# Sliding-window attention with a dense layer behind it: for 17 of 23 sessions the attention weights become the stationary operand, v with a column of ones the moving one, and x is transposed by SyncE's DMA

## The chip, the cores and the metric

The kernel runs on one core of one Trainium2 chip. Its time is the device time of one execution in microseconds (us); lower is better. TensorE (PE in the profile, its weight loads PEld) multiplies matrices, VectorE (DVE) and ScalarE (ACT) work element by element and read PSUM, GpSimd (POOL) here mostly issues the loads that convert float32 to bfloat16, and SyncE (SP) issues stores and DMA transposes.

## The reference

```python
# q, k, v: (8 batches, 8 heads, 576 tokens, 64)
scores = q @ k.transpose(0, 1, 3, 2) / sqrt(64)
scores = where(abs(i - j) <= 32, scores, -1e9)        # a band of 65 keys per query
attn   = softmax(scores)
x      = (attn @ v).transpose(0, 2, 1, 3).reshape(4608, 512)
h      = x @ w_in                                      # w_in: 512 x 2048
g      = where(h >= 1, h, where(h <= -1, 0, (h + 1)**2 / 4))
out    = g @ w_out                                     # w_out: 2048 x 512, float32
```

## The kernel before

All matrices are bfloat16 in SBUF; sums are float32 in PSUM. x is kept transposed: `xT` has its 512 features in four blocks of 128 partitions and its tokens along the free axis, in a ring of 4 x 576 tokens. `gT` is g transposed in the same manner, in four homes of 256 tokens.

**The main loop** runs over 144 steps `a` and after that over 16 more. A step projects hidden features of some tokens (`hp`, from `w_in` and `xT`: L609 for 256 features of 256 tokens, L630 for 128 features of 512 tokens in steps 56 to 135), then ACT and DVE make g of it (L648 to L655). A step also issues some of the matmuls of `g @ w_out` (`unit`, L563), whose number is written out by hand in the list `units`. Everything is in an order written out by hand; nothing is reordered by a scheduler, and each engine takes its instructions in order.

**Attention** runs ahead of the projection as a stream. From batch 1 on, the keys of all batches are cut into blocks of 64. Session k consists of `stream_sums(k)` and `stream_scores(k + 1)`; the list `sl` says in which step it runs. For the sessions that matter here the steps are: k = 6 in step 33, 7 in 36, 8 in 39, 9 in 44, 10 in 48, 11 in 51, 12 in 59, 13 in 66, 14 in 71, 15 in 74, 16 in 81, 17 in 87, 18 in 95, 19 in 99, 20 in 108, 21 in 111, 22 in 123. `stream_scores` multiplies k with q (L283) into PSUM, ACT takes the exponential (L289, L292) into the ring `wt` [keys of a block on 64 partitions, twice; queries along the free axis], DVE masks it (L200) and adds the two halves that belong to the same query into `rows` (L299). `stream_sums(k)` covers 192 queries: for each block of 64 keys it loads v as the stationary operand and moves `wt` past it (L366), so that the result comes out with the features of v on the partitions, which is what `xT` wants; and it moves `rows` past a block of ones to get the sums of the softmax on all partitions. Four 64x64 tiles of TensorE are used: `a`, the half of the partitions that the keys stand on, and `h`, the half of the partitions that the result goes to. `normal` then takes the reciprocal of the sums on ACT as exp(-ln(sum)) (L317, L320, L321), and its last step, a multiply on DVE that writes `xT` (L325), is put in the list `muls`, which `flush` issues at the start of the next step.

**Loads.** `load_nat` (L103) issues the loads of a batch's q and k on GpSimd's queue, `xpose` (L193) turns each with a DMA transpose on SP's queue once it has landed, `load_v` (L111) loads v. After the transpose of k, GpSimd copies two columns of kT to `gate` (L668); the copy waits until that transpose has landed, and the loads of v come behind it in GpSimd's order. Stores of results (`out_dram<-osb`, L571) are on SP's queue too. Tokens of batch b stand at 576 b in the ring; session k writes 192 tokens from 576 + 736 + 192 (k - 6) on. The first step that reads tokens of a session is 40 for k = 6 and 7, 48 for k = 8, 56 for k = 9 to 11, 72 for 12 and 13, 88 for 14 to 16, 104 for 17 to 19, 120 for 20 and 21, and 136 for 22.

Of the kernel before, what the change touches and what calls it, by code (L numbers as in the profile page):

```python
# [7 lines left out]
FP = mybir.dt.float32  # L8
BF = mybir.dt.bfloat16
# [5 lines left out]
def kernel(  # L15
# [19 lines left out]
    nc = tc.nc  # L35
    B, H, S, D = q.shape
    NT, DM, DFF = out.shape[0], 512, 2048
    NY = H // 2
    NC = S // 64
# [3 lines left out]
    TURN = 2 * NC  # L43
    STREAMS = (0, NC, 2), (NC, (B - 1) * NC, 3)
    RING = 4 * S
    PAD = 32
    WIDE = 56, 136
    LONG = 2
    SPLIT = range(20, 25)

    const = ctx.enter_context(tc.tile_pool(name="const", bufs=1))
    nat = ctx.enter_context(tc.tile_pool(name="nat", bufs=2))
# [9 lines left out]
    def two_banks(pool):  # L62
        return pool.tile([128, 2, 512], FP, name="bb", tag="bb")
# [8 lines left out]
    w_out = const.tile([128, 16, DM], BF, name="w_out")  # L72
    xT = const.tile([128, NY, RING], BF, name="xT")
    gT = const.tile([128, 16, 4, 256], BF, name="gT")
    qTs = [const.tile([128, PAD + NY * S], BF, name=f"qT{i}") for i in range(3)]

    ctx.enter_context(tc.manual_schedule())
# [7 lines left out]
    def load_half(half, t, h, eng=None, x=None):  # L85

        src, dst, nm = ((q, qn, "qh"), (k, kn, "kh"))[t]
        if (0, half) not in dst:
            dst[0, half] = early.tile([128, 2, S], BF, name=nm, tag=nm, bufs=2) if x is None else x
        (eng or nc.gpsimd).dma_start(out=dst[0, half][:, h], in_=src[0].rearrange(  # L90
            "(h y) (l p j) d -> h l p y (j d)", h=2, l=2, p=32)[h][half])

# [12 lines left out]

    def load_v(b, n):
        if b not in vn:
            vn[b] = nat.tile([128, 2 * NC, 2, D], BF, name="vn", tag="vn", bufs=3)
        h, a = divmod(n, 2)
        y = NY * h + 2 * a  # L110
        nc.gpsimd.dma_start(out=vn[b][64 * a:64 * a + 64, :, h], in_=v[b, y:y + 2].rearrange("y s d -> (y s) d")  # L111
                            .rearrange("(c r) d -> r c d", r=64))

    def load_w_in(c0, c1, h, parts=(0, 64)):
# [46 lines left out]
    def qkT(b, t):  # L161
        if t == 0:
            return qTs[b % 3][:, PAD:]
        if b not in kT:
            kT[b] = ktp.tile([128, NY * S], BF, name="kT")
        return kT[b]
# [98 lines left out]
    def stream_scores(k, eng, pool=ps_s):  # L265

        assert eng is not None
        s, gs = turns[k]
        m = len(gs)
        r0 = (gs[0] - s) % TURN  # L270
        ps = two_banks(pool)
        sp = list(spare()) if m == 3 else None

        def place(h, y, n):
            return sp[h][:, 1, 128 * y:128 * y + 128] if n == 2 else ps[:, h, 256 * y + 128 * n:256 * y + 128 * n + 128]

        for y, n in [(y, n) for y in range(2) for n in range(min(m, 2))] + [(y, 2) for y in range(2) if m == 3]:
            for a in range(2):
                for h in range(2):
                    b, c = 1 + gs[n] // NC, gs[n] % NC  # L280
                    lo, hi = 32 * (c == 0), TAIL if c == NC - 1 else 128
                    s0 = S * (y + 2 * a) + 64 * c
                    nc.tensor.matmul(place(h, y, n)[HD[a], lo:hi], kT[b][HD[h], s0:s0 + 64],  # L283
                                     qTs[b % 3][HD[h], PAD + s0 - 32 + lo:PAD + s0 - 32 + hi],
                                     start=True, stop=True, skip_group_check=True)
        w0 = 128 * r0
        lo, hi = 32 * (gs[0] % NC == 0), 128 * m - 32 * (gs[-1] % NC == NC - 1)
        cut = min(hi, 256)
        A.activation(wt[:, :, w0 + lo:w0 + cut], ps.rearrange("p h (y j) -> p (h y) j", y=2)[:, :, lo:cut], AF.Exp,  # L289
                     scale=D ** -0.5)  # L290
        for h in (1, 0) if m == 3 else ():
            A.activation(wt[:, 2 * h:2 * h + 2, w0 + 256:w0 + hi],  # L292
                         sp[h][:, 1].rearrange("p (y j) -> p y j", y=2)[:, :, :hi - 256], AF.Exp, scale=D ** -0.5)
        mask(eng, wt[:, :, w0 + lo:w0 + hi], mask4.rearrange("p (m j) -> p m j", m=4)[:, :, lo:hi])
        M = turn_of(k)
        r = rows[64 * gs[0] - 32] = ptp.tile([128, 4, 192], BF, name="rows", bufs=2)
        if r0:
            x = wt[:, :, w0 - 64:w0 - 64 + 128 * M].rearrange("p m (n e j) -> p m n e j", n=M, e=2)
            V.tensor_add(r[:, :, :64 * M].rearrange("p m (n j) -> p m n j", n=M), x[:, :, :, 0], x[:, :, :, 1])  # L299
        else:  # L300
            V.tensor_add(r[:, :, :64], wt[:, :, 128 * TURN - 64:], wt[:, :, :64])
            x = wt[:, :, 64:64 + 128 * (M - 1)].rearrange("p m (n e j) -> p m n e j", n=M - 1, e=2)
            V.tensor_add(r[:, :, 64:64 * M].rearrange("p m (n j) -> p m n j", n=M - 1), x[:, :, :, 0], x[:, :, :, 1])

    def turn_of(k):

        return next(m for s, e, m in STREAMS if s == turns[k][0])
# [3 lines left out]
    def normal(bb, w, parts, more=None):  # L311
# [14 lines left out]
                                                                   rc[:, :, :D0].rearrange(like, y=2)[:, :, :, x0:x1]))  # L326
        return end

    def stream_sums(k, pool=ps_n):

        bb = two_banks(pool)
        s, m, lo, hi = ranges[k]
        w = hi - lo
        t = 64 * s + 64 * m * ((lo - 64 * s + 32) // (64 * m)) - 32
        r, i = (rows[t], lo - t) if t in rows else (wt, 128 * ((t - 64 * s) // 64 % TURN) + 64)
        more = list(spare()) if w > 128 else None
        cut = min(4 * w, 512) - 2 * w
        todo = []
        for y in range(2):
            for g in range(max(s, lo // 64 - 1), min(hi // 64 + 1, (B - 1) * NC)):  # L340
                b, c = 1 + g // NC, g % NC
                u = 64 * g - 32
                q0, q1 = max(lo, u, S * (b - 1)), min(hi, u + 128, S * b)
                if q0 < q1:
                    todo.append(((b, NC * y + c), 2, y * w + q0 - lo, y * w + q1 - lo,
                                 lambda a, h, y=y, j=128 * ((g - s) % TURN) - u, q0=q0, q1=q1: wt[HD[a], 2 * h + y, j + q0:j + q1]))
        if more is None:
            todo.insert(0, (None, 2, 2 * w, 4 * w, lambda a, h: r[HD[a], 2 * h:2 * h + 2, i:i + w]))
        else:
            def ends(n0, n1):  # L350
                def get(a, h):
                    if w == 192:
                        return r[HD[a], 2 * h:2 * h + 2].rearrange("p y j -> p (y j)")[:, n0:n1]
                    return r[HD[a], 2 * h + n0 // w, i + n0 % w:i + n0 % w + n1 - n0]
                return get
            todo += [(None, 2, 2 * w + c0, 2 * w + c1, ends(c0, c1)) for c0, c1 in spans(0, cut, w)]
            todo += [(None, None, c0 - cut, c1 - cut, ends(c0, c1)) for c0, c1 in spans(cut, 2 * w, w)]
        seen = set()
        for c, where, c0, c1, p in todo:
            for a in range(2):  # L360
                for h in range(2):
                    o = bb[HD[h], a, c0:c1] if where else more[a][HD[h], 0, c0:c1]
                    if not c and more is None:
                        o = o.rearrange("p (y j) -> p y j", y=2)
                    key = (a, h, where)
                    nc.tensor.matmul(o, vn[c[0]][HD[a], c[1], h] if c else ones[HD[a]],  # L366
                                     p(a, h), start=key not in seen, stop=True, skip_group_check=True)
                    seen.add(key)
        t0 = S + lo
        cut = min(w, RING - t0 % RING)  # L370
        return normal(bb, w, [(x0, x1, (t0 + x0) % RING) for x0, x1 in ((0, cut), (cut, w)) if x0 < x1], more)
# [5 lines left out]
    def sums(b, y1, lo, hi, pool=ps_n):  # L377
# [23 lines left out]
        for n, (c, c0, c1, p) in enumerate(todo):  # L401
            o = D0 if c is None else 0
            for a in range(2):
                for h in range(2):
                    nc.tensor.matmul(bb[HD[h], a, o + c0:o + c1], ones[HD[a]] if c is None else vn[b][HD[a], c, h],
                                     p(a, h), start=n == 0, stop=True, skip_group_check=True)

        def end():
# [121 lines left out]
    for t, a in enumerate([7, 16]):  # L530
        xps.setdefault(a, []).append((2, t))
    for b in range(LONG + 1, B):
        a = [19, 26, 37, 60, 84][b - 3]
        for t in range(2):
            loads.setdefault(a + t, []).append((b, t))
        for t in range(2):
            xps.setdefault([[23, 24], [33, 34], [46, 48], [65, 69], [89, 91]][b - 3][t], []).append((b, t))

    op = {}

# [76 lines left out]
    for a in range(NF * NB + 2 * NF):  # L617
# [46 lines left out]
        run(a + 0.5)  # L664
        for x in xps.get(a, []):
            xpose(*x)
            if x[1]:
                P.tensor_copy(gate, qkT(x[0], 1)[:, 0:2])  # L668
                for n in range(4):
                    load_v(x[0], n)  # L670

# [29 lines left out]
```

## Time and profile before

| | us |
|---|---|
| three runs | 303.43, 303.51, 302.79; median 303.43 |
| span of the profiled execution | 303.0 (no other time of that execution is given; the three runs lie within 0.5 around it) |
| TensorE busy | 293.1 (97%) |
| VectorE, ScalarE, GpSimd busy | 232.0, 203.4, 78.8 |
| DMA moved | 35.66 MB |

Busy time is the time in which an engine has an instruction in work. In rows of groups the columns are line, engine, operation, tiles, shapes and count, then busy time in us and mean ns of one, then the idle time just before them and what ended it. In rows of the timeline they are start, length, engine, line, operation, count, and in brackets the idle time before and its releaser. In rows of waits they are who waited for whom, us in all, times, longest. Rows of SPq and POOL with DMA in them show the issue of a transfer, not its landing; the landing stands in a row of its own.

### The profile page before, as it was taken

To read this page: it belongs to the slowest core of one execution; us is meant where nothing else is said; L and a number is where in the kernel's file an instruction comes from. 1 tells how busy PE (TensorE), PEld (TensorE's weight loads), DVE (VectorE), ACT (ScalarE), POOL (GpSimd) and SP (SyncE) were. 2 spreads that over 40 slices of the span, in tenths; PEclk is the share of its full clock that TensorE was granted. 3 is DMA by queue.
4 is the path that set the end of the run, shared out by engine and by line. 5 is a ranking of instruction groups with operands and counts; after the bars stand their busy time and mean duration, and the time that the engine had idled before them with its cause. 6 is when DMAs were issued, how large, how long until landed. Compare 5 with 4: busy or idle time off the path is not lost.

```text
span 303.0 us, 7769 instructions
## 1 busy us (share of the span) xinstructions
PE 293.1 (97%) x3244; PEld 172.2 (57%) x3244; DVE 232.0 (77%) x361; ACT 203.4 (67%) x383; POOL 78.8 (26%) x98
## 2 busy tenths in 40 slices
PE   8788999999999999999999999999999999999995
PEld 3466888876665766644444444444444444446644
DVE  4269789989987889898988989688978887546700
ACT  3678696757786777766878487777578547685301
POOL 8794740090073046055046000050000000000000
PEclk9999999999999999999999999999999999999999
DMA  9999999999999999999989900697111110000121
GB/s 151 180 180 199 187 186 154 225 151 156 185 65 147 178 171 145 166 188 147 195 119 161 159 17 22 131 137 73 38 35 38 35 37 35 37 35 35 38 104 69
DMA packets 137971, 35.66 MB, mean 118 GB/s; under 512 B 122320, under 2 KB 134352, under 8 KB 137936
## 3 DMA queue, kind: packets, MB, share of 16 engines
q0 software_dynamic: 103056, 18.06, 81.0%
q1 hardware_dynamic: 34736, 16.81, 23.9%
q8 instruction: 25, 0.41, 0.6%
q10 hardware_dynamic: 144, 0.29, 0.4%
q14 instruction: 10, 0.08, 0.1%
HBM read 36.70 MB, written 9.44 MB: 152 GB/s over the span
## 4 chain that ended last, share of the span: by engine, by line
PE 82%; DMA 7%; POOL 5%; DVE 2%; ACT 2%; issue 1%; POOLq 0%; ACTq 0%; DVEq 0%
PE op L563 34%; PE hp L630 23%; PE hp L609 14%; PE op L581 4%; PE bb L366 3%; DMA w_out<-in_moe_w_out_dram 3%; DMA vn<-in_v_dram 2%; POOL w_in L116 2%; DMA w_in<-in_moe_w_in_dram 2%; POOL vn L111 2%; PE bb L283 1%; PE op L554 1%; DVE wt L200 1%; PE tp L186 1%; PE sp L366 1%
## 5 line engine op out<-in xcount | busy, mean ns | idle before, releaser
L648 ACT ACTIVATE rr<-hp 128x512 f32<-128x512 f32 x144 | 84.9, 594 | 67.0 <-PE hp L630 36.1
L563 PE MATMUL op<-w_out,gT 128*128 128x512 bf16 x496 | 125.5, 380 | 0.0
L654 DVE TENSOR_TENSOR mx<-hp,rr 128x512 f32<-128x512 f32 x104 | 71.2, 685 | 17.2 <-ACT rr L648 16.5
L630 PE MATMUL hp<-xT,w_in 128*128 128x512 bf16 x320 | 81.1, 379 | 0.0
L563 PEld LDWEIGHTS <-gT 128*128 128x128 bf16 x496 | 46.9, 98 | 49.8
L655 DVE SCALAR_TENSOR_TENSOR gT<-rr,mx 128x512 bf16<-128x512 f32 x104 | 72.2, 694 | 3.6
L609 PE MATMUL hp<-xT,w_in 128*128 128x256 bf16 x512 | 65.8, 273 | 2.6 <-DMA w_in<-in_moe_w_in_dram 1.7
L609 PEld LDWEIGHTS <-w_in 128*128 128x128 bf16 x512 | 48.9, 98 | 17.6 <-issue 3.0
L630 PEld LDWEIGHTS <-w_in 128*128 128x128 bf16 x320 | 31.3, 98 | 37.9 <-issue 0.2
L652 DVE SCALAR_TENSOR_TENSOR gT<-hp,mx 128x512 bf16<-128x512 f32 x40 | 27.5, 688 | 15.8 <-ACT mx L651 14.4
L668 POOL COPY gate<-kT 128x2 bf16<-128x2 bf16 x6 | 1.3, 224 | 113.6 <-DMA kT<-kn 113.6
L111 POOL DMA_DIRECT2D vn<-in_v_dram x32 | 27.3, 870 | 6.6 <-DVE gT L652 2.4
L651 ACT ACTIVATE mx<-rr 128x512 f32<-128x512 f32 x40 | 25.2, 630 | 1.3
L289 ACT ACTIVATE wt<-bb 128x1024 bf16<-128x1024 f32 (+2 forms) x23 | 22.1, 966 | 5.7 <-PE bb L283 5.7
L200 DVE TENSOR_TENSOR wt<-wt,mask 128x1408 bf16<-128x1408 bf16 (+4 forms) x23 | 19.5, 847 | 6.0 <-ACT wt L292 5.3
L325 DVE TENSOR_TENSOR xT<-bb,rc 128x768 bf16<-128x768 f32 (+4 forms) x25 | 20.5, 827 | 3.3 <-ACT rc L321 3.2
L567 ACT COPY osb<-op 128x512 f32<-128x512 f32 x23 | 13.3, 578 | 10.7 <-PE op L563 10.7
L321 ACT ACTIVATE rc<-rc 128x768 f32<-128x768 f32 (+4 forms) x24 | 18.3, 763 | 0.8
L581 PE MATMUL op<-w_out,gT 128*128 128x256 bf16 x128 | 16.1, 273 | 1.2 <-DMA w_out<-in_moe_w_out_dram 1.2
L103 POOL DMA_DIRECT2D qn<-in_q_dram x12 | 14.8, 1259 | 1.8 <-DMA kn<-in_k_dram 1.3
L103 POOL DMA_DIRECT2D kn<-in_k_dram x12 | 14.8, 1267 | 0.2 <-issue 0.2
L581 PEld LDWEIGHTS <-gT 128*128 128x128 bf16 x128 | 12.5, 98 | 2.8 <-issue 1.3
(82 smaller groups left out, 206.6 us busy)
## 6 DMA issues: line engine op xcount, KB each, us to landing
out_dram<-osb SPq DMA_DIRECT2D x30, 256.0 KB, 2.4
vn<-in_v_dram POOLq DMA_DIRECT2D x32, 144.0 KB, 5.0
qn<-in_q_dram POOLq DMA_DIRECT2D x12, 288.0 KB, 8.0
kn<-in_k_dram POOLq DMA_DIRECT2D x12, 288.0 KB, 9.8
out_dram<-osb SPq DMA_DIRECT2D x12, 128.0 KB, 1.7
w_in<-in_moe_w_in_dram POOLq DMA_DIRECT2D x11, 128.0 KB, 5.0
w_out<-in_moe_w_out_dram POOLq DMA_DIRECT2D x4, 256.0 KB, 9.5
w_out<-in_moe_w_out_dram POOLq DMA_DIRECT2D x2, 512.0 KB, 11.9
```

The lines of the kernel that those rows point to most:

```text
L103: nc.gpsimd.dma_start(out=x[:, :, h], in_=src[b, NY * h:NY * h + NY].rearrange("y s d -> (y s) d") .rearrange("(u p) d -> p u d", p=128))
L111: nc.gpsimd.dma_start(out=vn[b][64 * a:64 * a + 64, :, h], in_=v[b, y:y + 2].rearrange("y s d -> (y s) d") .rearrange("(c r) d -> r c d", ...
L200: eng.tensor_mul(p, p, m)
L563: nc.tensor.matmul(op[tt], gT[:, j, home(tt // 2), 128 * (tt % 2):128 * (tt % 2) + 128], w_out[:, j], start=j == 0, stop=j == 15)
L581: nc.tensor.matmul(o[:, tt], gT[:, j, p, 128 * tt:128 * tt + 128], w_out[:, j, 256 * half:256 * half + 256], start=not done, stop=len(done ...
L609: nc.tensor.matmul(hp[:, j], w_in[:, kk, 256 * f + 128 * j:256 * f + 128 * j + 128], xT[:, kk, r0:r0 + TB], start=first and n == 0, stop=l ...
L630: nc.tensor.matmul(hp.rearrange("p n t -> p (n t)"), w_in[:, kk, 128 * f:128 * f + 128], xT[:, kk, r0:r0 + 2 * TB], start=n == 0, stop=n == 3)
L648: A.activation(rr, hp, AF.Relu, scale=0.5, bias=0.5)
L651: A.activation(mx, rr, AF.Square)
L652: V.scalar_tensor_tensor(g, hp, 1.0, mx, op0=ALU.max, op1=ALU.min)
L654: V.tensor_max(mx, hp, rr)
L655: V.scalar_tensor_tensor(g, rr, 1.0, mx, op0=ALU.min, op1=ALU.mult)
```

## The change

For sessions 6 to 22 (`TURNED`) the product with v is turned round:

- v gets two more columns per block and head, which GpSimd sets to one once in each of three fixed buffers `vns` (before, v came from a pool of three).
- `turned_sums` loads 64x64 blocks of `wt` as the stationary operand and moves 65 columns of v past them: 64 features and one of the ones. The result has queries on the partitions, and the softmax's sum in column 64 beside them. There are 48 such matmuls for 192 queries, in place of 40.
- `rows` is not made for these sessions, and Ln and Exp on ACT go. DVE takes the reciprocal of 12 sums per partition and multiplies into `xn` (tokens on the partitions), in two parts of 512 and 256 elements.
- SP turns `xn` into `xT` by DMA transposes: one of 128 tokens by 512 features and two of 64 tokens by 256 (for k = 11, which passes the end of the ring, the first is cut in three).
- The tile q half `qh` has one buffer in place of two.
- Batch 4's transposes of q and k move from steps 33 and 34 to 37 and 38, and its loads of v are gated by the transpose of q in place of k; batch 5's loads move from step 37 to 39 and its transposes from 46 and 48 to 52 and 55; batch 6's transposes from 65 and 69 to 67 and 69.

```diff
+    TURNED = range(6, 23)
...
+    vns = [const.tile([128, 2 * NC, 2, D + 2], BF, name=f"vn{i}") for i in range(3)]
...
-            vn[b] = nat.tile([128, 2 * NC, 2, D], BF, name="vn", tag="vn", bufs=3)
+            vn[b] = vns[b % 3]
+            if 2 <= b < 5:
+                P.memset(vn[b][:, :, :, D:], 1.0)
...
         M = turn_of(k)
+        if k in TURNED:
+            return
         r = rows[64 * gs[0] - 32] = ptp.tile([128, 4, 192], BF, name="rows", bufs=2)
...
+    def turned_sums(k, pool=ps_n):
+        bb = two_banks(pool)
+        s, m, lo, hi = ranges[k]
+        g0 = (lo + 32) // 64
+        E = D + 1
+        todo = [(g0, e, 2 * y + h, y, h) for y in range(2) for h in range(2) for e in range(2)]
+        todo += [(g0 + 2, y, 4 + h, y, h) for h in range(2) for y in range(2)]
+        seen = set()
+        for part in (todo[:8], todo[8:]):
+            for back in (1, 0):
+                for g, e, n, y, h in part:
+                    c = g - back + (e if n < 4 else 0)
+                    j = 128 * ((c - s) % TURN) + 64 * back
+                    for a in range(2):
+                        nc.tensor.matmul(bb[HD[e], a, E * n:E * n + E], wt[HD[a], 2 * h + y, j:j + 64],
+                                         vn[1 + c // NC][HD[a], NC * y + c % NC, h, :E],
+                                         start=(a, e) not in seen, stop=True, skip_group_check=True)
+                        seen.add((a, e))
+        def scale():
+            rs = smp.tile([128, 2, 6], FP, name="rs")
+            x = bb[:, :, :6 * E].rearrange("p a (n e) -> p a n e", e=E)
+            V.reciprocal(rs, x[:, :, :, D])
+            xn = early.tile([128, 2, S], BF, name="xn", tag="kh", bufs=2).rearrange("p h s -> p (h s)")
+            parts = xn[:, :8 * D], xn[:, 8 * D:12 * D]
+            for p, n0, n1 in zip(parts, (0, 4), (4, 6)):
+                V.tensor_mul(p.rearrange("p (a n d) -> p a n d", a=2, d=D), x[:, :, n0:n1, :D],
+                             rs[:, :, n0:n1].rearrange("p a (n e) -> p a n e", e=1).to_broadcast([128, 2, n1 - n0, D]))
+            t0 = (S + lo) % RING
+            cuts = (32, 64) if RING - t0 == 32 else ()
+            for p0, p1 in zip((0, *cuts), (*cuts, 128)):
+                r0 = (t0 + p0) % RING
+                nc.sync.dma_start_transpose(out=xT[:, :, r0:r0 + p1 - p0], in_=parts[0][p0:p1])
+            r0 = (t0 + 128) % RING
+            for y in range(2):
+                nc.sync.dma_start_transpose(out=xT[:, y::2, r0:r0 + 64], in_=parts[1][HD[y]])
+        return lambda: muls.append(scale)
...
-        a = [19, 26, 37, 60, 84][b - 3]
+        a = [19, 26, 39, 60, 84][b - 3]
...
-            xps.setdefault([[23, 24], [33, 34], [46, 48], [65, 69], [89, 91]][b - 3][t], []).append((b, t))
+            xps.setdefault([[23, 24], [37, 38], [52, 55], [67, 69], [89, 91]][b - 3][t], []).append((b, t))
...
-            if x[1]:
-                P.tensor_copy(gate, qkT(x[0], 1)[:, 0:2])
+            if x[1] == (x[0] != 4):
+                P.tensor_copy(gate, qkT(*x)[:, 0:2])
```

More of the change, by code (lines that the diff above doesn't have):

```diff
@@ L88, in load_half @@
         if (0, half) not in dst:
-            dst[0, half] = early.tile([128, 2, S], BF, name=nm, tag=nm, bufs=2) if x is None else x
+            dst[0, half] = early.tile([128, 2, S], BF, name=nm, tag=nm, bufs=1 + t) if x is None else x
         (eng or nc.gpsimd).dma_start(out=dst[0, half][:, h], in_=src[0].rearrange(
@@ L107, in load_v @@
         if b not in vn:
-            vn[b] = nat.tile([128, 2 * NC, 2, D], BF, name="vn", tag="vn", bufs=3)
+            vn[b] = vns[b % 3]
+            if 2 <= b < 5:
+                P.memset(vn[b][:, :, :, D:], 1.0)
         h, a = divmod(n, 2)
         y = NY * h + 2 * a
-        nc.gpsimd.dma_start(out=vn[b][64 * a:64 * a + 64, :, h], in_=v[b, y:y + 2].rearrange("y s d -> (y s) d")
+        nc.gpsimd.dma_start(out=vn[b][64 * a:64 * a + 64, :, h, :D], in_=v[b, y:y + 2].rearrange("y s d -> (y s) d")
                             .rearrange("(c r) d -> r c d", r=64))
@@ L327, in normal @@
         return end
+    def turned_sums(k, pool=ps_n):
[34 more added lines that the diff above has]
+        return lambda: muls.append(scale)
     def stream_sums(k, pool=ps_n):
+        if k in TURNED:
+            return turned_sums(k, pool)
         bb = two_banks(pool)
@@ L365, in stream_sums @@
                     key = (a, h, where)
-                    nc.tensor.matmul(o, vn[c[0]][HD[a], c[1], h] if c else ones[HD[a]],
+                    nc.tensor.matmul(o, vn[c[0]][HD[a], c[1], h, :D] if c else ones[HD[a]],
                                      p(a, h), start=key not in seen, stop=True, skip_group_check=True)
@@ L404, in sums @@
                 for h in range(2):
-                    nc.tensor.matmul(bb[HD[h], a, o + c0:o + c1], ones[HD[a]] if c is None else vn[b][HD[a], c, h],
+                    nc.tensor.matmul(bb[HD[h], a, o + c0:o + c1], ones[HD[a]] if c is None else vn[b][HD[a], c, h, :D],
                                      p(a, h), start=n == 0, stop=True, skip_group_check=True)
```

## The prediction

> **What bounds the kernel now.** I read the page first, then who TensorE waited for, then busy time by stretches.
>
> ```profile
> span 303.0 us, 7769 instructions
> PE 293.1 (97%) x3244; PEld 172.2 (57%) x3244; DVE 232.0 (77%) x361; ACT 203.4 (67%) x383; POOL 78.8 (26%) x98
> PE 82%; DMA 7%; POOL 5%; DVE 2%; ACT 2%; issue 1%; POOLq 0%; ACTq 0%; DVEq 0%
> ```
> ```profile
> PE hp L609 <- DMA w_in<-in_moe_w_in_dram: 1.7, 2, 1.0
> PE bb L366 <- DMA vn<-in_v_dram: 0.7, 1, 0.7
> ```
> ```profile
> 87.00:100.00 13.00, 12.32 (x198) 8.29 (x196) 10.27 (x16) 9.46 (x21) 6.83 (x7) 1.00 2.38 135
> 100.00:303.00 203.00, 199.93 (x1846) 104.55 (x1843) 154.73 (x229) 132.31 (x255) 29.13 (x32) 1.00 0.75 94
> ```
>
> TensorE is busy 97% of the span and carries 82% of the chain that ended last. In the stretches (columns: length, then busy PE, PEld, DVE, ACT, POOL, granted clock, DMA share) it works 199.93 of the last 203 us, at clock 1.00, while DVE and ACT have 48 and 71 us to spare. Of its waits only one lies in the part the change touches: 0.7 us for v inside a sums group. So work taken from ACT or DVE buys nothing by itself; what counts is TensorE's own time in a session, and any new wait.
>
> **TensorE in a session.** A session is one call of stream_sums (L366) with one of stream_scores (L283). The 17 changed ones are k = 6 to 22, the first near 80 us, the last at 251 us.
>
> ```profile
> 119.70:120.22 0.52, 0.51 (x40) 0.47 (x40) 1.00 2.41 152
> ```
> ```profile
> 119.70 0.38 PEld L366 LDWEIGHTS <-vn 64*64 64x64 bf16 x32 [0.21 <-issue]
> 67.17 0.32 PE L366 MATMUL bb<-wt,vn 64*64 64x64 bf16 x16
> 284.78 11.65 PE op L563 x54
> ```
>
> The 40 matmuls of sums in k = 11 fill 0.52 us: 32 with v (768 columns for each of four 64x64 tiles) and 8 with the ones (384 columns). The four tiles run side by side: 11.65 us / 54 / 512 = 0.42 ns a column gives 1152 x 0.42 = 0.48 us, close to the 0.52. After the change there are 48 matmuls, twelve rounds of four, with 65 columns each: 780 x 0.42 = 0.33 us, if loading new weights 48 times stays hidden. The second row bounds that: 16 matmuls, rounds of 64, 96, 64 and 96 columns, take 0.32 us with the last one's own latency of about 0.2 us, so three rounds start within some 0.12 us, 37 ns each at most. Twelve rounds then cost between 0.33 us (columns) and 0.44 us (37 ns). I take 0.36, nearer the column end, because a mean round there had 75 columns = 31 ns of work already. Gain 0.16 us a session (0.08 to 0.19), 17 x 0.16 = 2.7 us (1.4 to 3.2).
>
> By the Trainium skill, "TensorE: Matmul & The Clock Gate", section LDWEIGHTS, a weight load takes its columns divided by 1.2 in ns, 53 ns for 64, which would make twelve rounds 0.64 us and each session 0.12 us longer. The trace disagrees: 32 loads in 0.38 us, the last one's 0.1 us included, are seven rounds in 0.28 us, 40 ns, with 96 columns to stream in a mean round.
>
> **ACT and DVE.**
>
> ```profile
> L317 ACT ACTIVATE rc<-bb 128x256 f32<-128x256 f32 (+3 forms) x24 | 10.4, 433 | 0.4 <-PE bb L366 0.4
> L320 ACT ACTIVATE rc<-sp 128x256 f32<-128x256 f32 (+1 forms) x36 | 12.3, 417 | 0.0
> L321 ACT ACTIVATE rc<-rc 128x768 f32<-128x768 f32 (+4 forms) x24 | 18.3, 763 | 0.8
> L299 DVE TENSOR_TENSOR rows<-wt 128x768 bf16<-128x768 bf16 (+1 forms) x19 | 10.1, 530 | 0.7
> L325 DVE TENSOR_TENSOR xT<-bb,rc 128x768 bf16<-128x768 f32 (+4 forms) x25 | 20.5, 827 | 3.3 <-ACT rc L321 3.2
> ```
>
> ACT loses L317, two of L320 and L321, about 0.43 + 2 x 0.34 + 0.84 = 1.9 us a session, 33 us in all. DVE loses L299 (0.56) and L325 (0.96) and gets a reciprocal of 12 elements (0.1 to 0.2) and two multiplies of 512 and 256 elements; at L325's rate of about 1.25 ns an element 0.65 and 0.35, so DVE gains some 0.3 us. I cost both at nothing: no wait of TensorE after 100 us hangs on either. POOL gets three memsets of 144 bytes a partition ahead of v loads; their nearest row, the gate copy, took 0.18 us.
>
> **The new path of x.** xT used to be written by L325. Now the product goes to xn, and SP turns it: per session one DMA of four 128x128 blocks and two of two half blocks, together 6 of the 18 blocks of a q or k transpose (one session, k = 11, uses five DMAs).
>
> ```profile
> 192.18 2.54 SPq L193 DMA_TRANSPOSE qT<-qn  x1
> ```
> ```profile
> DMA to landing us min/median/max: 4.8/4.8/4.8
> ```
> ```profile
> out_dram<-osb SPq DMA_DIRECT2D x30, 256.0 KB, 2.4
> ```
> ```profile
> L571 SPq DMA_DIRECT2D out_dram<-osb x1: 332/332/332, 139.9 to 139.9; - x1
> DMA to landing us min/median/max: 6.2/6.2/6.2
> ```
>
> With no loads about, a whole q transpose is issued in 2.54 us and lands 4.8 after its issue began (the second fence is L193 alone between 190 and 200 us). The four blocks therefore take 4/18 x 2.54 = 0.6 us to issue and land 2.3 us later, 2.9 us in all. Amid a stream of GpSimd's loads it is another matter: the store issued at 139.9 us, while batch 6's q and k were loading, landed after 6.2 us, against 2.4 at the median. It looks as if an SP transfer stands behind the load descriptors already handed out. I take 2.9 us where loads are drained and 5.5 to 6.5 us amid them.
>
> "DMA: Bandwidth & Descriptors" of the Trainium skill, section Queues, rings and completion order, says that an engine takes turns between its queues packet by packet; the transposes would then land soon even amid loads. The 6.2 us speak against it.
>
> **Who reads it first.** The first reader of k's tokens sits at a fixed place in TensorE's order. Most are 12 to 32 us after the session; four are not.
>
> ```profile
> 85.58 3.41 POOL L111 DMA_DIRECT2D vn<-in_v_dram  x4 [0.85 <-PE hp L609]
> 88.93 2.49 POOL L103 DMA_DIRECT2D qn<-in_q_dram  x2
> 91.35 2.48 POOL L103 DMA_DIRECT2D kn<-in_k_dram  x2
> 87.54 0.54 PE L366 MATMUL bb<-wt,vn 64*64 64x64 bf16 x32
> 89.99 0.89 DVE L200 TENSOR_TENSOR wt<-wt,mask 128x1408 bf16<-128x1408 bf16 x1 [0.30 <-ACT wt L292]
> 95.39 0.45 PE L366 MATMUL bb<-wt,vn 64*64 64x96 bf16 x24 [0.68 <-DMA vn<-in_v_dram]
> 97.82 1.04 PE L609 MATMUL hp<-xT,w_in 128*128 128x256 bf16 x8
> ```
> ```profile
> L103 POOL DMA_DIRECT2D kn<-in_k_dram x2: 1277/1282/1286, 91.4 to 92.5; - x2
> DMA to landing us min/median/max: 8.6/9.1/10.0
> ```
>
> k = 7 (87.54): the mask ends at 90.88, reciprocal and first multiply end near 91.7, SP issues at 91.6 to 91.9 (the session itself comes 0.3 earlier). The reader is step 40, at 97.82: 6 us to land, in the middle of batch 4's loads. At 5.5 to 6.5 us that is a wait of 0 to 0.6; at 7.5, halfway from the store's 6.2 to the 8.6 of the quickest load there, 1.6. I take 0.4. Ahead of it k = 8 waits for batch 3's v until 95.39. TensorE reaches that wait 0.32 us earlier but leaves it no earlier, so the gain of k = 6 and 7 is lost there; and k = 6's transposes (6/18 of 2.54 = 0.85 us of queue) go out just ahead of that v: 0 to 0.85, I take 0.2.
>
> ```profile
> 97.90 0.96 DVE L200 TENSOR_TENSOR wt<-wt,mask 128x1536 bf16<-128x1536 bf16 x1 [1.26 <-ACT wt L292]
> 99.12 3.52 SPq L193 DMA_TRANSPOSE qT<-qn  x1
> 103.43 2.90 SPq L193 DMA_TRANSPOSE kT<-kn  x1
> 109.96 0.18 POOL L668 COPY gate<-kT 128x2 bf16<-128x2 bf16 x1 [16.13 <-DMA kT<-kn]
> 111.83 1.03 PE L609 MATMUL hp<-xT,w_in 128*128 128x256 bf16 x8
> ```
>
> k = 8: its product is ready near 99.7, but on SP its transposes now stand behind batch 4's qT and kT (steps 37 and 38), which wait for their loads. That is 106.3 plus some 0.4, so issue at 106.7. Meanwhile the gate no longer waits for kT, so v of batch 4 starts near 105.6 instead of 110.5, beside kT and these transposes. Landing 110 (2.9 us behind a kT that landed at 109.9) to 113 (6.2 us). The reader, step 48, was at 111.83, about 112.2 with the delays above: 0 to 0.8, I take 0.3. The same move drops no wait of TensorE, since v of batch 4 came in time before.
>
> ```profile
> 128.28 1.03 PE L630 MATMUL hp<-xT,w_in 128*128 128x512 bf16 x4
> ```
> ```profile
> 207.69 0.54 PE L366 MATMUL bb<-wt,vn 64*64 64x64 bf16 x32
> 210.15 0.89 DVE L200 TENSOR_TENSOR wt<-wt,mask 128x1408 bf16<-128x1408 bf16 x1 [0.28 <-ACT wt L292]
> 216.21 1.03 PE L630 MATMUL hp<-xT,w_in 128*128 128x512 bf16 x4
> ```
>
> k = 11 (119.7, reader 128.28) and k = 19 (207.69, reader 216.21) have 8.5 us. Mask end at +3.35, product 0.85 later, issue at +4.4, landing at +7.3: some 1 us to spare with the loads drained, so nothing. Batches 5 and 6 get their q and k some 3 us later, with over 10 us before their first scores; their stores and transposes on SP pass k = 11 to 13's without a reader near. Nothing.
>
> **Sum.** 15 sessions x 0.16 = -2.4; v of batch 3 +0.2; step 40 +0.4; step 48 +0.3: -1.5 us on a span of 303.03. The three runs were 302.79 to 303.51, the span lies among them; against their median, 303.43, I forecast 301.9. About 0.3%, 0.9 us, is what a measurement can tell from no change.
>
> **Rivals.**
> 1. Transposes held back until the load stream is drained. For: kn, issued by 92.55, landed 10.0 us later, at 102.5, and q and k transposes in the trace were all issued only once their loads had landed, so none shows how one fares inside a stream. Then k = 7's lands near 102.5 and step 40 waits 4.7 us; step 48 then waits no more. 303.43 - 2.4 + 0.2 + 4.7 = 305.9. It decides from a landing 3.3 us past step 40. Against: the store at 139.9 did get through. Chance 0.20.
> 2. The same waits, only larger than I took: v +0.85, step 40 +1.0, step 48 +0.8: 303.43 - 2.4 + 2.65 = 303.7, no change (302.5 to 304.3). Chance 0.18.
> 3. Weights not hidden: sessions 0.12 us longer, 17 x 0.12 = +2.0, with the waits 306.3 (304.5 upward). The 40 ns of the weight row speak against it. Chance 0.05.
> 4. Queues share evenly, no wait at steps 40 and 48: 303.43 - 2.4 = 301.0, with 0.19 a session 300.2. The page named above says so; the late store speaks against it. Chance 0.12.
>
> The forecast (300.9 to 302.5) has 0.45. Faster 0.45 + 0.12 = 0.57, same 0.18, slower 0.25. Range 300.2 to 306.0, which leaves out a tenth at each end at most.
>
> **What would show it.** L366's successor in a session near 0.36 us and 48 loads; no L320 or L321 between 80 and 250 us; idle time of TensorE named "DMA xT" at step 40 and 48 only, under 1 us each; transposes of xT landing in about 2.9 us after 200 us and in 5 to 7 near 92 us. I am wrong if the session does not get shorter, or if TensorE waits for xT over 3 us in sum.

## The result, and the profile after

The changed kernel is slower: 318.07 us at the median of four runs (314.57 to 320.69) beside 303.47 (302.79 to 304.05), ratio 1.038, 95% interval 1.031 to 1.045. A second series of the same kernel gave 314.2 (312.74 to 315.32), ratio 1.032 (1.024 to 1.039). The prediction was 301.9, range 300.2 to 306.0. The first ratio leaves out the two longest of the four runs, 320.69 (the profiled one) and 319.96, which lie over 1.5% above the fastest; a second profile, of an execution of 315.31 in the second series, therefore stands beside the first below and carries the reading.

From the page of the changed kernel, first profile: the span, TensorE's and DVE's busy time, the chain that ended last, and the granted clock in 40 slices.

```profile
span 318.9 us, 8092 instructions
PE 290.7 (91%) x3349; PEld 171.6 (54%) x3380; DVE 227.1 (71%) x375; ACT 178.6 (56%) x315; POOL 79.1 (25%) x101
PEclk9999999999999987999995999999999999999999
PE 58%; DMA 5%; DVE 2%; issue 1%; ACT 1%; SPq 0%; DVEq 0%; ACTq 0%
```

The 290.7 us is too low: this trace holds 3349 matmuls beside 3380 weight loads (PEld), and each matmul of these kernels has its own load, so 31 records are missing. The second profile has them all:

```profile
PE 295.2 (94%) x3380; PEld 171.9 (55%) x3380; DVE 226.8 (72%) x375; ACT 178.7 (57%) x315; POOL 80.2 (26%) x101
```

TensorE's busy time thus rose by 2.1 us, and its share fell from 97% to 94%: it now stands still at times. The clock row, 9 in every slice before, has dips. Who TensorE waited for, first profile and then the second:

```profile
PE hp L657 <- DMA xT<-xn: 6.1, 1, 6.1
PE hp L678 <- DMA xT<-xn: 4.9, 2, 3.3
PE bb L350 <- DMA vn<-in_v_dram: 1.2, 1, 1.2
```
```profile
PE hp L657 <- DMA xT<-xn: 4.4, 2, 4.2
PE hp L678 <- DVE xn L362: 2.4, 1, 2.4
PE bb L350 <- DMA vn<-in_v_dram: 2.0, 2, 1.3
```

L657 is the projection of 256 features (before L609), L678 that of 512 tokens (before L630). The 6.1 and the 4.2 are step 48, reading k = 8's tokens; the 4.9 and the 2.4 are step 72, reading k = 13's. (The 2.4 is put down to DVE, whose multiplies feed the transposes; TensorE went on at 165.39, just after k = 13's second transpose, which landed at 165.25.) Timeline of TensorE at step 48 and busy time by stretches there, second profile:

```profile
116.58 1.86 PE L657 MATMUL hp<-xT,w_in 128*128 128x256 bf16 x8 [4.19 <-DMA xT<-xn]
```
```profile
112.00:117.00 5.00, 0.81 (x6) 0.32 (x5) 1.38 (x2) 0.60 (x1) 3.91 (x5) 0.74 2.54 138
117.00:121.00 4.00, 4.00 (x82) 2.36 (x81) 1.38 (x2) 1.92 (x4) 1.05 (x1) 0.50 2.17 162
121.00:126.00 5.00, 5.00 (x34) 3.27 (x33) 4.34 (x8) 1.82 (x4) 0.00 (x0) 0.97 2.15 137
```

Those eight matmuls took 1.03 us before and take 1.86 now: for the four microseconds behind the pause the granted clock is 0.50. So this wait is paid about one and a half times. The pause of 2.4 us at step 72 ends in the same way, at a clock of 0.62 from 166 to 170 us:

```profile
162.00:166.00 4.00, 1.57 (x7) 0.47 (x8) 3.43 (x7) 1.49 (x3) 0.00 (x0) 0.95 2.29 189
166.00:170.00 4.00, 4.00 (x13) 1.58 (x12) 1.39 (x2) 1.70 (x3) 0.00 (x0) 0.62 1.28 170
```

Setting the start of each weight load of the second profile against the same load of before gives the account of its 10 us. TensorE is 1.2 us ahead until batch 3's v makes it wait and 0.35 late when that v has come; it loses 0.5 at step 40, 4.5 at step 48, 1.8 more at half clock, 2.8 at step 72, and 1.4 more at half clock. The turned sessions give back 0.1 each, and it ends 9.8 late.

### The profile page after: what moved, and what is told of

The parts are those of the page before. It is cut to its first block, busy times and chain, and to the rows that moved or that the text cites. A ratio compares the mean times of both kernels' runs of the same rounds, so it can differ in the third digit from the quotient of the medians.

```text
span 318.9 us, 8092 instructions
## 1 busy us (share of the span) xinstructions
PE 290.7 (91%) x3349; PEld 171.6 (54%) x3380; DVE 227.1 (71%) x375; ACT 178.6 (56%) x315; POOL 79.1 (25%) x101
## 4 chain that ended last, share of the span: by engine, by line
PE 58%; DMA 5%; DVE 2%; issue 1%; ACT 1%; SPq 0%; DVEq 0%; ACTq 0%
PE op L611 27%; PE hp L678 21%; PE hp L657 6%; DMA xT<-xn 5%; PE bb L350 2%; PE op L602 1%; PE bb L287 1%; DVE mx L702 1%; DVE gT L703 1%; PE sp L287 0%; ACT rr L696 0%; DVE xn L362 0%; DVE wt L204 0%; SPq L371 0%; DVE gT L700 0%
## 5 line engine op out<-in xcount | busy, mean ns | idle before, releaser
L611 PE MATMUL op<-w_out,gT 128*128 128x512 bf16 x472 | 121.2, 381 | 3.3 <-issue 3.2
L678 PE MATMUL hp<-xT,w_in 128*128 128x512 bf16 x315 | 82.6, 385 | 5.2 <-DMA xT<-xn 4.9
L657 PE MATMUL hp<-xT,w_in 128*128 128x256 bf16 x512 | 66.6, 275 | 10.4 <-DMA xT<-xn 6.1
L657 PEld LDWEIGHTS <-w_in 128*128 128x128 bf16 x512 | 49.1, 98 | 26.1 <-issue 10.1
L678 PEld LDWEIGHTS <-w_in 128*128 128x128 bf16 x320 | 31.5, 99 | 44.2 <-issue 7.5
L362 DVE TENSOR_TENSOR xn<-bb,rs 128x512 bf16<-128x512 f32 (+1 forms) x34 | 17.4, 553 | 0.6
L629 PEld LDWEIGHTS <-gT 128*128 128x128 bf16 x128 | 12.5, 98 | 1.5
L350 PEld LDWEIGHTS <-wt 64*64 64x64 bf16 x816 | 8.6, 109 | 7.4 <-issue 7.4
```

The costliest lines, as they stand in the source:

```text
L611: nc.tensor.matmul(op[tt], gT[:, j, home(tt // 2), 128 * (tt % 2):128 * (tt % 2) + 128], w_out[:, j], start=j == 0, stop=j == 15)
L629: nc.tensor.matmul(o[:, tt], gT[:, j, p, 128 * tt:128 * tt + 128], w_out[:, j, 256 * half:256 * half + 256], start=not done, stop=len(done ...
L657: nc.tensor.matmul(hp[:, j], w_in[:, kk, 256 * f + 128 * j:256 * f + 128 * j + 128], xT[:, kk, r0:r0 + TB], start=first and n == 0, stop=l ...
L678: nc.tensor.matmul(hp.rearrange("p n t -> p (n t)"), w_in[:, kk, 128 * f:128 * f + 128], xT[:, kk, r0:r0 + 2 * TB], start=n == 0, stop=n == 3)
```

## The experiments

Names in the expectations: Q says that transposes of xT come late, behind loads and SP's other work; P that the new places cost by themselves; T that the 65-column tiles lower the clock; H that the clock halves when TensorE has stood still; O that SP's order alone decides. An x transpose is a transpose of a session's x, from `xn` to `xT`.

**Without the transposes.** DVE multiplies straight into `xT`, which then holds features and tokens mixed (k = 11 is left unturned).

```diff
-            xn = early.tile(...)
...
-                nc.sync.dma_start_transpose(...)
+                V.tensor_mul(xT[...], x[:, e, 0:4, :D]..., r[...])
```


> Theory Q (queues): the turned sums themselves save 0.15 us a session, and all that is lost is TensorE waiting for xT, whose transposes stand behind GpSimd's loads and behind the q and k transposes on SP. This kernel keeps the turned sums of sessions 6 to 22 without 11, and the new places, but DVE multiplies straight into xT and no transpose of x is issued (so the layer behind reads features and tokens mixed; the amount of work is the same). Q expects TensorE to wait for no xT, and 16 x 0.15 = 2.4 us less than before: about 301, at clock 1.00. Theory P (places): the re-placed transposes and loads of q and k make TensorE late, so the waits near steps 48 and 72 stay in another form and the time stays above 306. Theory T (tiles): short 65-column matmuls with new weights each time let the clock drop; then clock stays under 0.99 and the time above 304.

303.1 us (10 runs) beside 303.6, ratio 0.999 (0.997 to 1.002). There is no wait for xT and the clock is 1.00; from 60 us on TensorE's longest wait is

```profile
PE bb L350 <- DMA vn<-in_v_dram: 1.0, 1, 1.0
```

The loss is therefore in the transposes and what they cause; T falls. The gain that Q hoped for, 2.5 us, is not there either: half a microsecond, within the interval.

**The places alone.** No session is turned, the new places stay.

```diff
-    TURNED = range(6, 23)
+    TURNED = ()
```


> No session is turned; v's three fixed buffers and the new places of batches 4 to 6 stay. Theory Q expects the time of before, 303 to 304.5: the q and k transposes have 10 us and more to spare. Theory P expects most of the 14.6 us, so over 310. Theory T expects the time of before.

304.35 (10 runs), ratio 1.004 (1.001 to 1.007). P explains 0.75 us of the loss, by the interval 2 us at most. Against this kernel the one without transposes is 1.25 us faster, of the size that its 16 sessions should bring at 0.11 each (1.8).

**The old places.** All 17 sessions turned, batches 4, 5 and 6 where they were.

> All 17 sessions turned with their transposes of x, but batches 4 to 6 at the places of before. Theory Q: on SP the transposes of x of sessions 6 and 7 now stand behind q and k of batch 4, which wait for their loads until some 106 us; step 40 reads k = 7's tokens at 97.8 us, so TensorE waits there 14 us or more, in one piece, and the time is 318 or worse. Theory P: the places were the loss, so 301 to 304.

327.63. Its waits:

```profile
PE hp L657 <- DMA xT<-xn: 15.1, 1, 15.1
PE hp L678 <- DMA xT<-xn: 5.7, 1, 5.7
```

Step 40 waits 15.1 us, because k = 7's transposes now stand behind kT of batch 4 on SP; step 56 waits 5.7. The new places are thus a remedy for something worse, as Q expected.

**Batch 4's v behind kT again.** One condition of the change is undone.

```diff
-            if x[1] == (x[0] != 4):
-                P.tensor_copy(gate, qkT(*x)[:, 0:2])
+            if x[1]:
+                P.tensor_copy(gate, qkT(x[0], 1)[:, 0:2])
```


> Only batch 4's gate goes back from the q transpose to the k transpose, so that its loads of v start some 4 us later, behind kT. Theory Q: kT and k = 8's transposes no longer share the queues with those loads; xT of k = 8 lands near 114 in place of 118.9, the wait of 6.5 us at step 48 shrinks to 1 to 2 us and the 2 us at half clock after it go: 310 to 313, if step 72 keeps its wait. If the wait came from SP's order alone (kT ahead of k = 8 on SP), step 48 keeps 5 us or more and the time stays at 315 to 320.

315.05 (4 runs), ratio 1.038 (1.033 to 1.043), where Q had 310 to 313. k = 8's first transpose, issue to landing: the changed kernel's second profile, then this one.

```profile
DMA to landing us min/median/max: 6.4/6.4/6.4
```
```profile
DMA to landing us min/median/max: 2.5/2.5/2.5
```

It is the same transfer behind the same kT on the same queue (issued at 110.10 and 109.65); only the four loads of v beside it are gone, and the wait at step 48 goes from 4.2 to 0.3 at most. O falls here: with SP's order unchanged the wait is gone. The loads of v, put off, are paid for elsewhere:

```profile
PE bb L350 <- DMA vn<-in_v_dram: 5.1, 4, 2.8
PE hp L678 <- DMA xT<-xn: 2.6, 1, 2.6
PE hp L678 <- DVE rs L358: 1.8, 1, 1.8
```

**Filling the pause.** Twenty matmuls of no use ahead of step 48.

```diff
+            if a == 48:
+                z = ps_h.tile([128, 512], FP, name="z", tag="hp")
+                for _ in range(20):
+                    nc.tensor.matmul(z, w_out[:, 0, :128], w_out[:, 1], start=True, stop=True)
```


> The changed kernel with 20 matmuls of 512 columns on w_out, whose result nobody reads, put ahead of step 48's projection: 20 x 0.216 = 4.3 us of work inside the 6.3 us that TensorE stands still there. Theory H (TensorE's clock halves after it has stood still for some us): the idle stretch falls to 2 us, and the 4.4 us at clock 0.50 behind step 48 go, about 1.9 us of time; the clock dip behind step 72 stays. If the dips come from something else (the chip, the run), the dip behind step 48 stays and the time too, within the 2 to 3 us that single runs of the changed kernel differ.

312.99. Around the fill (at 113.5 to 118):

```profile
113.00:118.00 5.00, 4.95 (x27) 2.48 (x26) 1.42 (x3) 0.60 (x1) 4.59 (x4) 1.00 2.05 170
118.00:122.00 4.00, 3.84 (x94) 2.73 (x94) 2.37 (x4) 2.11 (x5) 0.27 (x1) 1.00 2.70 137
```

The fill takes 4.3 us, about as long as the wait of 4.2 it covers, and the clock stays at 1.00 behind it, so H holds at step 48. The time of this one run lies among the changed kernel's own (312.7 to 315.3) and shows no gain. "TensorE: Matmul & The Clock Gate" of the Trainium skill, section Part 1: The HAM clock gate, says that the clock halves when TensorE has idled for about 3.4 us and is restored after as long a time of work. The trace agrees at step 48, where the 4.2 us pause ended at 0.50 for some 4 us. It does not agree on the length: 2.4 us were enough at step 72. In other runs 2.1 us at batch 3's v (the kernel with nine late sessions below) and 2.8 us at batch 4's v (the kernel above with v behind kT) were each followed by 3.4 us of half clock, and so were 1.4 us at batch 3's v in the run with the fill; 2.6 us at step 56 of the kernel with v behind kT were not. From 3.0 us on every pause in these traces was followed by it; what decides below that stays open. The prediction did not reckon with the clock.

**Batch 4's kT after k = 8.**

```diff
-[37, 38]
+[37, 40]
```


> Batch 4's transpose of k moves from step 38 to 40, which on SP puts it behind the transposes of x of session 8. Theory O (SP's order alone): xT of session 8 now goes out some 4.4 us earlier, the length of kT's issue; step 48 finds it, kT lands in time for the scores at 48 or 2 us late, and the kernel gains 5 us or more. Theory Q (SP's and the queues' capacity between 100 and 120 us is short: q 5.2 us of issue, k 4.4, two sessions of x 3.7 each, and loads beside them): the wait moves to the scores of step 48, which then wait for kT 4 us or more, and the time stays within 3 us of 318.

319.67. SP now takes the x transposes first, at 105.84, and kT at 110.83; step 48's scores pay:

```profile
PE bb L287 <- DMA kT<-kn: 6.2, 1, 6.2
PE hp L678 <- DMA xT<-xn: 4.4, 1, 4.4
```

Whichever goes first on SP, the other one's reader waits.

**Fewer sessions.** Ten (9, 10, 12, 14, 15, 17, 18, 20 to 22) in the old places; and fifteen, without 8 and 13, in the new ones.

> Ten sessions turned (9, 10, 12, 14, 15, 17, 18, 20, 21, 22), those whose first reader stands 14 us or more behind them and which SP does not hold up; all else at the places of before. Theory Q: no wait for xT, ten times 0.15 = 1.5 us less, 302, ratio 0.995 (0.992 to 0.999). If transposes of x also delay the loads of v, q and k enough, a wait for v or kT of 1 to 3 us appears near 120 us and it comes out at 303 to 306.

> The changed kernel with sessions 8 and 13 taken back to the old way (DVE writes their xT), everything else and the new places kept. Theory Q with the two waits belonging to these sessions' own tokens: the waits of 6.5 us at step 48 and 5.7 us at step 72 go with their half-clock tails, the time falls to 304 to 306. If the stage as a whole is short of queue time, step 48's scores wait for kT (115.5 us in the changed kernel, wanted at 113 to 114) 1.5 to 3 us, step 56 or 72 waits for another session's tokens, and it stays at 308 to 313.

314.87 (5 runs), ratio 1.036 (1.032 to 1.040), where Q had 302; and 311.24 (4 runs), ratio 1.025 (1.018 to 1.032). SP in the kernel with ten, and TensorE's longest wait:

```profile
125.75 3.55 SPq L197 DMA_TRANSPOSE qT<-qn  x1
129.47 2.73 SPq L197 DMA_TRANSPOSE kT<-kn  x1
132.29 1.22 SPq L368 DMA_TRANSPOSE xT<-xn  x1
133.61 2.46 SPq L371 DMA_TRANSPOSE xT<-xn  x2
```
```profile
PE hp L678 <- DMA xT<-xn: 5.6, 2, 4.1
```

k = 10 is caught behind batch 5's qT and kT, as k = 8 was behind batch 4's, and step 56 waits 4.1 and then 1.5 us. In the kernel without 8 and 13 step 56 waits too (4.3 us), for k = 11, whose five transposes were issued from 125.18 to 131.99 amid the loads of batch 5's q and k and landed after 4.4 to 8.1 us. In the changed kernel that step does not wait: in its second profile step 48 had held everything up, so that k = 11's transposes went out from 130.86 on, when the last of those loads was landing (131.40), and landed after 2.3 to 2.8 us. So the waits hide each other, and taking out the sessions that showed one doesn't remove the loss. Both sets followed the waits of one trace; that was the miss.

**Only the late sessions**, 14 to 22, with the old places.

> Only k = 14 to 22 are turned, with the places of the kernel before; k = 6 to 13 are computed as before. Theory Q (the loss is made where transposes of xT meet a reader soon behind batch 3 to 6's loads or their transposes; elsewhere the turned session keeps its gain): no wait for xT, nine sessions x 0.15 = -1.35 us: about 302.1 beside a kernel before of 303.5, ratio 0.995 to 0.997. Rival (each x transpose costs something wherever it is, through DMA traffic or SP): no gain or a loss, ratio 1.00 to 1.01, with waits spread after 170 us.

303.93 (12 runs) beside 303.3, ratio 1.001 (0.997 to 1.004): no change, where Q had 302.1. TensorE waits for no transpose. Transposes landing after 212 us, with loads drained, and k = 20's sums followed by its scores, here and before:

```profile
DMA to landing us min/median/max: 2.4/2.4/2.5
```
```profile
231.57 0.58 PE L350 MATMUL bb<-vn,wt 64*64 64x65 bf16 x48
231.97 0.40 PE L287 MATMUL bb<-qT,kT 64*64 64x128 bf16 x16
```
```profile
230.31 0.54 PE L366 MATMUL bb<-wt,vn 64*64 64x64 bf16 x32
230.84 0.39 PE L283 MATMUL bb<-qT,kT 64*64 64x128 bf16 x16
```

From the first sum to the first score a turned session takes 0.40 us, before 0.53. Over the nine sessions TensorE gains 0.9 us in this trace, 0.10 each; what it had lost by then, 1.9 us, it lost near 95 us, ahead of the first turned session, at batch 3's v and the half clock behind that. The wait for this v was 2.1 us, before 0.7, mainly because TensorE came there 1.1 us earlier: the v itself landed at 95.65, before at 95.35. In the other kernels with the new buffers for v it landed at 94.3 to 96.2, so no run shows that the buffers delay it. With this loss the gain cannot be told from none.

**One transpose a session**, the last 64 tokens multiplied straight into `xT`; **plain copies** of the same bytes in place of transposes; and **k = 8's transposes on ScalarE's queue**.

```diff
-            r0 = (t0 + 128) % RING
-            for y in range(2):
-                nc.sync.dma_start_transpose(out=xT[:, y::2, r0:r0 + 64], in_=parts[1][HD[y]])
```


> All 17 sessions turned, all places of the changed kernel, but the last 64 tokens of a session are multiplied straight into xT without a transpose (their values are left in the wrong layout), so SP issues one x transpose a session in place of three. If SP's issue time (1.2 us each, 3.7 us a session) is what makes the transposes late: the wait at step 48 falls by 2.4 us to about 4, those at step 72 vanish (the first of k = 13 landed 3.9 us ahead of its last), about 309. If the landing amid loads (7 to 9 us for the first one too) and kT's place on SP are what matters: step 40 still waits about 1, step 48 about 5 to 6, only step 72's fall, 311 to 314.


```diff
-                nc.sync.dma_start_transpose(out=xT[:, :, r0:r0 + p1 - p0], in_=parts[0][p0:p1])
+                nc.sync.dma_start(out=xT[:, :, r0:r0 + p1 - p0], in_=parts[0]...[:, :, p0:p1])
```


> The changed kernel with each x transpose replaced by a plain copy of the same bytes from xn to xT on the same queue (the values land untransposed), so that only the kind of transfer changes. If it is transposing that is slow: issue near 0.5 us, landing in about 2.5 us even amid loads, waits at steps 40, 48 and 72 under 2 us in sum, about 303. If any SP transfer amid GpSimd's loads lands late, as the stores do (6 to 8 us): issue shorter, step 48 still waits 3 to 6 us behind kT, step 72 1 to 4, 308 to 316.


```diff
+            eng = nc.scalar if k == 8 else nc.sync
```


> The changed kernel, but k = 8's three transposes are issued by ScalarE's queue, so they do not stand behind qT and kT of batch 4 on SyncE's; ScalarE's own instructions wait behind them for some 4 us. If SP's order makes step 48 late: they are issued near 100 to 104 and land, 7 to 8 us later amid the loads, near 108 to 112; the wait of 6.1 us at step 48 falls under 1 us and the half clock behind it goes; later readers (step 56) then come out earlier and may wait in its place, as when the gate was put back. 308 to 313. If the load stream holds them whoever issues them: landing stays near 118, step 48 still waits about 6, 318.

307.75, 308.82 and 328.36. k = 8's transfer with one transpose, and k = 7's with plain copies, amid the loads:

```profile
DMA to landing us min/median/max: 7.1/7.1/7.1
```
```profile
L368 SPq DMA_DIRECT2D xT<-xn x1: 613/613/613, 90.3 to 90.3; - x1
DMA to landing us min/median/max: 8.0/8.0/8.0
```

A plain copy is issued in 0.61 us, where a transpose needs 1.2, and lands no earlier amid loads. So the late landing is not the transposing; it is any SP transfer there. What both kernels save over the changed one's second series, 5 to 6 us in one run each, fits SP's shorter time: step 48 waits 2.3 and 3.3 us longer than before, step 72 1.2 and nothing. With one transpose no wait is followed by a half clock, with plain copies one is, the 3.0 us at step 48, for 3.4 us.

The run on ScalarE's queue told something else:

```profile
112.02 1.30 ACTq L369 DMA_TRANSPOSE xT<-xn  x1
116.01 0.60 ACT L697 ACTIVATE rr<-hp 128x512 f32<-128x512 f32 x1 [19.20 <-DMA xT<-xn]
```

The transpose is issued just after kT has landed (111.77). Until then ScalarE stands at waits of the program, put down to the same line, for the semaphores of qT's and kT's transfers; so the program itself keeps the transposes of two queues apart, and the run does not show what the chip would do without these waits. ScalarE stood still for 19.2 us behind it, and TensorE waited 16 behind it in turn. Its question, whether a queue of its own would help k = 8, stays open.

**One transpose, and v behind kT.** Last, the two remedies together.

> One transpose a session as in the run above that left out the other two (the last 64 tokens in the wrong layout), and batch 4's v gated on kT again. If landing amid v's loads is what still costs 2.3 us at step 48: k = 8's transpose lands 2.5 us after its issue, in place of 7.1, and step 48 waits for nothing; v of batch 4 then comes later and k = 10 or 11 waits 1 to 3 us for it: 305 to 308 in all. If it is SP's order that costs it, behind kT: step 48 waits 2 us as before, 307 to 309.

306.19, and k = 8's transpose, issued at 109.68:

```profile
DMA to landing us min/median/max: 2.5/2.5/2.5
```

Step 48 no longer waits; 0.5 to 1.6 us are left at each of batch 3's and 4's v, steps 40, 56 and 72. Single runs of the kernel before reach 306 too, so this one run is not told apart from it. And the changed kernel's second series:

> The changed kernel itself once more, for a second profile of it. If the waits found in the first profile are its ordinary cost: 314 to 320, with waits for xT at steps 40, 48 and 72 again, of 1 to 2, 3 to 6 and 2 to 6 us, and half clock behind those that are over some 3 us. If they were an accident of one execution: under 310, or waits at other places.

314.2, with the waits and the half clock shown above. The loss is its ordinary cost. No version that ran beats the kernel before.

## Why the prediction was wrong, point by point

- **What bounds the kernel** was right: work taken off ACT (203.4 to 178.6 us busy) and DVE (232.0 to 227.1) bought nothing, a new wait cost all.
- **A session's gain** was right: I took 0.36 us for twelve rounds and a gain of 0.16 (0.08 to 0.19); it measured 0.40, and the gain 0.10 to 0.14, in the lower half of the range. Twelve rounds in 0.40 us are 33 ns each. That is again under 53 ns, the estimate worked out from "TensorE: Matmul & The Clock Gate" of the Trainium skill, section LDWEIGHTS.
- **SP's issue time** was wrong. I scaled the 2.54 us of an 18-block transpose to 0.6 for four blocks and 0.85 for a session. Each takes about 1.2 us, however small:

```profile
100.47 5.08 SPq L197 DMA_TRANSPOSE qT<-qn  x1
105.64 0.53 SPq L619 DMA_DIRECT2D out_dram<-osb  x1
106.28 3.72 SPq L197 DMA_TRANSPOSE kT<-kn  x1
110.10 1.22 SPq L368 DMA_TRANSPOSE xT<-xn  x1
111.41 2.48 SPq L371 DMA_TRANSPOSE xT<-xn  x2
```

  This is SP in the second profile: 3.7 us a session, four times the forecast (k = 11 has five, 6.3 us).
- **Step 48** is the step that failed. I had k = 8's transposes issued from 106.7 and landed at 110 to 113, and took a wait of 0.3 into the sum; it cost 4.5 us, and 1.8 more at half clock. They were issued from 110.10 to 113.89 and landed at 116.45 to 118.97; step 48 read at 116.58. Three terms were too small. qT and kT ran 5.08 and 3.72 us on SP in place of 3.52 and 2.90, and later. Their loads came later: with k = 6 and 7's transposes beside them batch 4's two loads of k landed 12.5 and 12.7 us after their issue, where it had been 9.3 and 10.0 (the 8.6 of the prediction's row is a load of q); in the kernel with the old places, which had no x transposes there, 9.3 and 9.9. And v's loads, let go earlier, lay upon the landing: 6.4 us in place of 2.5. I had seen that they run "beside kT and these transposes", and yet kept the drained 2.9 us as one end.
- **Batches 5 and 6, "without a reader near. Nothing."** was wrong. GpSimd's copy that waits for kT of batch 5, with the places alone and then in the changed kernel's second profile:

```profile
131.46 0.19 POOL L716 COPY gate<-kT 128x2 bf16<-128x2 bf16 x1 [15.27 <-DMA kT<-kn]
```
```profile
146.92 0.18 POOL L716 COPY gate<-kT 128x2 bf16<-128x2 bf16 x1 [28.88 <-DMA kT<-kn]
```

  The moved steps alone do not make kT late; the transposes do: those of k = 9 to 11, 4.8, 4.0 and 6.3 us of SP, stand ahead of it, and TensorE itself is 7 us behind by then. The loads behind that copy, batch 5's v and batch 6's q and k, start 15 us later than before and meet k = 13's transposes; these landed after up to 8.3 us (9.2 in the first profile), and step 72 waited 2.4 (4.9).
- **Landing**: 2.3 to 2.5 us after the start of the issue drained, where I had 2.9 (0.6 and 2.3): right, with some to spare. Amid loads 5.9 to 10.0 (k = 7 to 10, 13 and 15 in the second profile), where I had 5.5 to 6.5: one late store carried the estimate, and it was the short end.
- **Step 40 and v of batch 3**: forecast +0.4 and +0.2; 0.5 and 1.6 in the second profile, 1.4 and 0.6 in the first. Right in kind, short in size.
- **The clock** was in no step. It added some 3.2 of the 10 us (1.8 + 1.4).
- **The rivals.** Rival 1 (305.9) had the mechanism, transposes held back by loads, at the wrong reader: step 40 waited 0.5, and where it said that step 48 "then waits no more" the loss lay. Rival 4, queues that share evenly, fell: 6.4 to 8.0 us amid loads, 2.5 without. Rival 3 fell with the 33 ns.
- **The base.** I put before's span, 303.0, among the runs, since no time of that execution was given. In the later runs the time is about 1.8 above the span, so it was an execution of about 304.8, longer than the median; gains counted against it look 1.3 us larger than they are. The kernel without transposes shows it: 1.8 us ahead in the trace, 0.5 at the median.

## What to carry to other kernels

A step handed to a DMA queue is to be costed by the queue's time for one such transfer (here about 1.2 us for each small transpose) and by a landing measured amid the loads that run at that time, not by a drained one; then the slack of each reader is what decides, and here step 40 had 6 us and its transpose took 7.7. Behind a first wait reckon with a half clock (here some waits under 3 us brought it, and all of 3.0 us or more), and then go through the later places once more, since the loads that stood clear of them have moved too. And waits found in one trace can hide others: leave all of the suspected part out first (one run showed here that transposes were the whole loss) before picking at single ones.

## What the runs showed of the hardware

- A DMA transpose occupied SP for about 1.2 us, for four 128x128 blocks as for two half blocks, while 18 blocks took 2.5 us with nothing beside them; amid loads single ones took up to 3.5. A plain copy of the first size took 0.61.
- SP transfers, plain or transposing, landed some 6 to 10 us after their issue amid GpSimd's loads (transposes 5.9 to 10.0 in the second profile, plain copies of k = 7 to 9 5.9 to 8.3) and 1.9 to 2.5 without; batch 4's loads of k beside them went from 9.3 and 10.0 us to 12.5 and 12.7.
- A pause of 4.2 us left TensorE at 0.50 of its clock for about 4 us; covered by matmuls of no use, it did not. Pauses of 1.4, 2.1, 2.4 and 2.8 us were each followed by half clock too, one of 2.6 us was not.
